# Seven block products of a gated feed-forward, accumulated in PSUM onto copies instead of added by VectorE

## The chip, the cores and the metric

One core of one Trainium2 chip. The metric is the device time of one execution in microseconds, median of three. In the texts, PE is TensorE (matmuls), PEld its weight loads, DVE is VectorE, ACT is ScalarE, POOL is GpSimd, SP the engine that issues most DMAs.

## The reference

```python
xn = layernorm(x)                              # x: 2048 x 512
s  = linear_attention(xn) @ wo                 # 32 heads of 16, dual softmax features
gate, up = xn @ W_gate, xn @ W_up              # 512 x 1376 each
h  = (gate * (gate > 0)) * up
out = x + s * silu(h @ W_down)                 # 1376 x 512
```

## The kernel before

All large products run in pairs of halves: every operand is split into a high part and a rest (`split`, L193: ScalarE writes the high part, VectorE or GpSimd subtracts to get the rest), and a product is three matmuls per block of the contraction (`mm3`, L198: rest times high, high times rest, high times high), accumulated in one PSUM bank of 128x512.

The kernel has three parts. First a loop over 16 tiles of 128 tokens: layer norm, transposes, the key, value and query projections, the feature map and the attention state. Then two passes (`half` 0 and 1, L1204), each over two blocks of 512 tokens. A pass walks 11 strips of the feed-forward width (`f` from 0 to 10, L1206). Each strip calls `gate_up(f)` (L558), which makes gate and up for both 512-token blocks. After the strips, a pass closes with the down projection of the last chunk of strips and the attention's output product (L1236 to L1276).

**`gate_up`.** Gate and up for the two token blocks form a 2x2 block product. The kernel uses seven block products instead of eight, on sums and differences of the inputs (A11, A12, A22, S1 to S4, kept in `XT`) and of the weights (`wa`, `wb`, `wc`, `wd`). Each product is two `mm3` steps, six matmuls of 512 columns. Before the change the order is: A11 into `pa`; S2 into `pb`; S3 into `pc`; S1 into `pd`; A22 onto `pc`; A12 onto `pa`; S4 onto `pd`. Three of them continue a bank that TensorE has written (`first=False`). What the banks must share is added by VectorE: a ScalarE copy `t1` of `pa`, then `m = pb + t1` (L571), `e7 = pc + m` (L582, or a ScalarE copy of `pc` when `copied`, that is in pass 1 from strip 2 on, with a GpSimd addition later, L593), `e7 = pd + e7` (L587), `pc = pc + m` (L594), `e7 = max(pc, 0) * e7` (L600), `m = pd + m` (L605) and `m = max(pa, 0) * m` (L606). The two results are split for the down projection; the split of the second one is put off (`LATE`) until the next strip's first product has been issued (`last_split`, L565). In a trace the tiles `t1`, `m` and `e7` show as `t`, `u` and `e`.

`gate_up` is a generator with seven yields, one after each product. `run` (L1186) steps through it, calls `pace.pump()` after each yield, and after the yields 3, 5, 6 and 7 issues one step of the down projection of earlier strips, if any is pending: two strips by three matmuls into a bank `py`, then an addition into `Y` (`y_sum`, L627: VectorE in pass 0, a ScalarE copy and GpSimd in pass 1). Such steps are pending in strips 2 to 9 of both passes, and not in the strips 0, 1 and 10: `CHUNKS` groups the strips by two, and `drain` (L1218) empties the list ahead of strip 10.

**What sets the order of the rest.** `Clock` (L62) keeps an estimate of when each engine is free, in TensorE cycles. `pump` issues pieces of other work (generators added with `pace.add`) when the estimate says that the engine is not more than `LIMIT` ahead. In pass 0 this is the preparation of the next strips' weights (`f_prep`, L479, on ScalarE and GpSimd, stored to HBM), the attention state (`state`, L1119: its results go over ScalarE as `XT<-kvt` and `zB<-pz`), and the queries (`q_pair`, L662: on VectorE a transpose `pq<-pql`, two reductions `mx`, two subtractions `eq`, later sums `qs`, reciprocals, two scalings `eq<-eq,qr` and transposes `ez` or `peT`; on ScalarE the exponentials and the copies `pTh`). In pass 1 the weights are reloaded from HBM and the queries go on. `InOrder` (L45) makes every engine issue in exactly the order in which the program was written, so whatever stands ahead of an instruction on its engine has to start first.

Of the kernel before, what the change touches and what calls it, by code (L numbers as in the profile page):

```python
# [13 lines left out]
P = 128  # L14
# [23 lines left out]
LATER = 9  # L38
START = (12, 15)
WO_WITH = (4, 5, 6, 7)  # L40

A21, A22, A11, A12, S1, S2, S3, S4 = range(8)

# [18 lines left out]
class Clock:  # L62
# [21 lines left out]
    def issued(self, key, name, a, k):  # L84
        o, ins = a[0], [*a[1:], *k.values()]
        n = max(x.free_size() for x in [o, *ins] if hasattr(x, "free_size"))
        start = max([self.now, *(self.there(x) + 200 for x in ins)])
        if name == "dma_start":
            self.ready[o.name] = start + self.LANDING
            if key == "gpsimd":  # L90
                self.free[key] = max(start, self.free[key]) + self.ISSUE
            return
        cost = self.RATE[key] * n
        if key == "tensor":
            n = o.free_size()
            cost = max(n, 245) + 30
            if name == "matmul" and a[2].dtype == F32:
                cost = n * 3 + 460
        if name == "reciprocal":
            cost *= 6  # L100
        self.free[key] = max(start, self.free[key]) + self.FIXED[key] + cost
        self.ready[o.name] = self.free[key] + (380 if key == "tensor" else 0)
# [56 lines left out]
def layer_kernel(ctx: ExitStack, tc: tile.TileContext, x, wkT, wqT, wv, wo, wf, cst, out):  # L159
# [46 lines left out]
            if i < n - 1:  # L206
                pace.pump()

    def transpose(o, src):
        nc.tensor.transpose(o, src, ident)  # L210

    def flat(e):
        return e.rearrange("p h s f -> p (h s f)")
# [29 lines left out]
    def fold(w, raw, k):  # L243

        p = ps(name="pfold")
        for j in range(KD):
            nc.tensor.matmul(p[:, j * P:(j + 1) * P], raw[:, j * P:(j + 1) * P], bd_sb[:, j, :],
                             start=True, stop=True)
        if w is WQ:
            return lambda: split(*w[k], p)  # L250
        return lambda: split(*map(by_parity, w[k]), even_first(p))
# [46 lines left out]
    def transpose_x(n):  # L298
        p = ps((P, 2, 2, P), name="pxT")
        xn = XN.pop(n)  # L300
        for k in range(KD):
            transpose(p[:, k // 2, k % 2, :], xn[:, k * P:(k + 1) * P])
        return p

    def xt_part(n, s):
# [58 lines left out]
    def query(n):  # L364


        h, d = divmod(n, 4)
        c = slice(h % 2 * 2 * P, (h % 2 + 1) * 2 * P)

        qs = [2 * b + h % 2 for b in PAIRS[h // 2][::-1]]  # L370
        p = ps((P, 2, 2 * P), name="pq")

        def w_of(d):
            return lambda k: [t[:, d * P:(d + 1) * P] for t in WQ[k]]
        if n < 2:
            i = 1 - n
            for d in range(2):
                mm3(p[:, d, :], w_of(d), lambda k: [XT[:, 2 * i + k // 2, s, k % 2, c] for s in range(2)], range(KD))
            to = [((qs[i], 0), slice(None), slice(None))]
        else:  # L380
            mm3(p, w_of(d), lambda k: [XT[:, k // 2:k // 2 + 3:2, s, k % 2, c] for s in range(2)], range(KD))
            to = [((q, d // 2), d % 2, i) for i, q in enumerate(qs)]
        t = u2((P, 2, 2 * P), "pqs")
        nc.scalar.activation(t, p, AF.Copy)
        for q, col, part in to:
            if q not in PQ:
                PQ[q] = dram((P, 2, 2 * P), f"pq{q[0]}{q[1]}")
            pace.when(t, lambda q=q, col=col, part=part: nc.sync.dma_start(PQ[q][:, col, :], t[:, part, :]))
# [166 lines left out]
    def a_of(c):  # L555
        return lambda k: (XT[:, c, 0, k, :], XT[:, c, 1, k, :])

    def gate_up(f, copied, used, halfway):  # L558

        pa = ps(name="pa")  # L560
        mm3(pa, w_of(f, 0, 0), a_of(A11), range(2))
        used(A11)
        t1 = u2((P, BT), "t1")
        nc.scalar.activation(t1, pa, AF.Copy)
        last_split()  # L565
        yield
        pb = ps(name="pb")
        mm3(pb, w_of(f, 1, 0), a_of(S2), range(2))
        used(S2)
        m = u2((P, BT), "u2")  # L570
        add(nc.vector, m, pb, t1)  # L571
        yield
        pc = ps(name="pc")
        mm3(pc, w_of(f, 1, 1), a_of(S3), range(2))
        FT[f][1] = None
        used(S3)
        halfway()
        e7 = u2((P, BT), "e7")
        if copied:
            nc.scalar.activation(e7, pc, AF.Copy)  # L580
        else:
            add(nc.vector, e7, pc, m)  # L582
        yield
        pd = ps(name="pd")
        mm3(pd, w_of(f, 2, 0), a_of(S1), range(2))
        used(S1)
        add(nc.vector, e7, pd, e7)  # L587
        yield
        mm3(pc, w_of(f, 2, 1), a_of(A22), range(2), first=False)
        FT[f][2] = None  # L590
        used(A22)
        if copied:
            add(nc.gpsimd, e7, e7, m)  # L593
        add(nc.vector, pc, pc, m)  # L594
        yield
        mm3(pa, w_of(f, 0, 1), a_of(A12), range(2), first=False)
        FT[f][0] = None
        used(A12)
        h1 = u2((P, BT), "hh", F32R), u2((P, BT), "hl", F32R)
        nc.vector.scalar_tensor_tensor(e7, pc, 0.0, e7, op0=ALU.max, op1=ALU.mult)  # L600
        split(*h1, e7, nc.gpsimd)
        yield
        mm3(pd, w_of(f, 3), a_of(S4), range(2), first=False)
        used(S4)
        add(nc.vector, m, pd, m)  # L605
        nc.vector.scalar_tensor_tensor(m, pa, 0.0, m, op0=ALU.max, op1=ALU.mult)  # L606
        h0 = u2((P, BT), "hh", F32R), u2((P, BT), "hl", F32R)
        LATE.append(lambda: split(*h0, m, nc.gpsimd))
        FT.pop(f)
        HS[f] = [h0, h1]  # L610
        yield
# [191 lines left out]
    def q_back(u, es, ez):  # L803

        (q, _), _ = UNITS[u]
        for j in range(2):
            th, tl = yield from turned_parts(u, es, ez, j, [(es[j], 0)])
            ez[j] = None
            yield "tensor", tl
            os_ = flat(es[j]).rearrange("p (a s t) -> p a s t", a=2, s=2)  # L810
            vh, vl = (t.rearrange("p (d t a x) -> p d a t x", d=2, a=2, x=32) for t in (th, tl))
            for a in range(2):
                p = ps((P, 2, 256), name="pnum")
                for s in range(2):
                    g = 4 * a + 2 * j + s
                    o = p[:, s, :].rearrange("p (t x) -> p t x", x=32)
                    mm(o, kvhl[:, 1, g, :], vh[:, s, a], True, False)
                    mm(o, kvhl[:, 0, g, :], vl[:, s, a], False, True)
                nc.scalar.activation(os_[:, a], p, AF.Copy)
            es[j] = None  # L820
            del th, tl, vh, vl
            DONE_Q[u] += 1
            STORES[u].append(pace.when(os_, lambda j=j, os_=os_: [o_store(q, j, s, os_[:, :, s, :]) for s in range(2)]))
        yield None,
# [361 lines left out]
    def run(g, per=1):  # L1186
        n = 0
        for _ in g:
            pace.pump()
            n += 1  # L1190
            if pending and n in (3, 5, 6, 7):
                if next(pending[0], pending) is pending:
                    pending.pop(0)
                    if pending:
                        next(pending[0])
                pace.pump()
# [7 lines left out]
    for half in range(2):  # L1204
        b0, b1 = 2 * half, 2 * half + 1
        for f in range(NF):  # L1206
# [21 lines left out]
            def used(c):  # L1228
                if half == 0 and f == NF - 1:
                    nc.sync.dma_start(f32(XT[:, c]), xt_spill[:, c - 1])  # L1230
            run(gate_up(f, half and f > 1, used, lambda: again and f_reload(f + 1, 1)))
            for c, fs in enumerate(CHUNKS[:-1]):
                if f == fs[-1]:
                    pending.extend(down((b0, b1)[j], j, fs, c == 0) for j in (1, 0))
# [7 lines left out]
        for j, b in enumerate((b1, b0)):  # L1242
            j = 1 - j
            if b == b0:
                for q in QUERIES[half][:2]:
                    o_split(q)
            parts = {}
            for i in range(TPB):
                if j == 1 and i < 3:
                    parts[i] = ps(name="py")  # L1250
                    down_rows(parts[i], i, j, fs[:-1], True, False)
            for i in range(TPB):
                if i in parts:
                    down_rows(parts[i], i, j, fs[-1:], False, True)
                else:
                    parts[i] = ps(name="py")
                    down_rows(parts[i], i, j, fs, True, True)
                y_sum(b, i, parts[i], False, True)
                y = Y[b][:, i, :]
                nc.scalar.activation(y, y, AF.Silu)  # L1260
                if b * TPB + i in yspill:
                    pace.when(y, lambda t=b * TPB + i, y=y: nc.sync.dma_start(yspill[t], y))
                pace.pump()
# [69 lines left out]
```

## Time and profile before

| what | us |
|---|---|
| median of three runs | 563.97 (563.05 to 564.35) |
| span of the profiled execution | 561.1 |
| start of the first strip of pass 1 in that span | 355.1 |
| last matmul in that span | 557.1 |

The profiled execution has no time of its own beside its span: 561.1 us lie between its first and its last instruction, 2.9 us less than the median of the runs. A change of the span is taken over to the median as it is. In the profile all instructions have line 58, that of the helper that records them, so they are told apart by their tiles: `pb<-XT,wb` is a matmul into `pb` from `XT` and `wb`. Rows of the timeline have the start in us, the duration in us, the engine, the operation, its tiles and shapes, how many instructions are merged in the row, and in brackets the idle time ahead of it and who ended it. Matmuls are pipelined: the duration of one row is longer than the distance to the next.

### The profile page before, as it was taken

What the parts mean: (1) busy time and instruction counts of PE and PEld (TensorE: products, weight loads), DVE (VectorE), ACT (ScalarE), POOL (GpSimd) and SP (SyncE); (2) the same over time, 40 slices, a digit from 0 to 9 for tenths busy, and PEclk for the clock granted to TensorE, in tenths of its full rate; (3) what the DMA queues carried; (4) which work ended last, traced back from release to release, by engine and by line L of the source; (5) the groups of instructions that cost most, each with busy time, mean ns of one, the idle gap of its engine ahead of it and who ended that gap; (6) DMA issues with size and microseconds to landing.
All of it is one profiled execution on the core that took longest, in us unless ns stands there. A gap on an engine that the chain in (4) does not pass through costs nothing.

```text
span 561.1 us, 8204 instructions
## 1 busy us (share of the span) xinstructions
PE 556.3 (99%) x2618; PEld 466.0 (83%) x2618; DVE 412.0 (73%) x623; ACT 282.7 (50%) x504; POOL 416.2 (74%) x356
## 2 busy tenths in 40 slices
PE   9999999999999999999999999999999999999997
PEld 8888888888888888888888888888888888888886
DVE  5978777677656898999798432699995959775324
ACT  3898687765545456444425251234463544534500
POOL 1689987898888386998889242572879788888474
PEclk9999999999999999999999999999999999999999
DMA  8349999765599827979767899997475666659675
GB/s 282 136 150 245 274 277 330 213 167 166 150 297 314 327 77 276 326 270 324 263 240 230 246 356 419 401 374 282 137 225 178 219 204 206 207 166 284 170 237 193
DMA packets 84538, 137.98 MB, mean 246 GB/s; under 512 B 7824, under 2 KB 34320, under 8 KB 83600
## 3 DMA queue, kind: packets, MB, share of 16 engines
q1 hardware_dynamic: 81040, 125.33, 65.1%
q0 software_dynamic: 3312, 12.06, 11.0%
q8 instruction: 21, 0.34, 0.3%
q14 instruction: 21, 0.17, 0.1%
q10 hardware_dynamic: 144, 0.07, 0.0%
HBM read 76.87 MB, written 52.69 MB: 231 GB/s over the span
## 4 chain that ended last, share of the span: by engine, by line
PE 99%; DVE 0%; issue 0%
PE py L58 21%; PE pc L58 11%; PE pa L58 11%; PE pd L58 11%; PE pv L58 8%; PE pk L58 8%; PE pq L58 8%; PE pso L58 8%; PE pb L58 5%; PE pkv L58 3%; PE pnum L58 3%; PE pxT L58 1%; PE pfold L58 1%; PE pidle L58 1%; PE pz L58 0%; DVE yk L58 0%
## 5 line engine op out<-in xcount | busy, mean ns | idle before, releaser
L58 PE MATMUL py<-fdh,hl 128*128 128x512 f32 x176 | 68.5, 389 | 0.0
L58 PE MATMUL py<-fdh,hh 128*128 128x512 f32 x176 | 68.5, 389 | 0.0
L58 PE MATMUL py<-fdl,hh 128*128 128x512 f32 x176 | 68.5, 389 | 0.0
L58 PE MATMUL pa<-XT,wa 128*128 128x512 f32 x264 | 67.4, 389 | 0.0
L58 POOL TENSOR_TENSOR hl<-e,hh 128x512 fp32r<-128x512 f32 x22 | 28.5, 1296 | 44.9 <-ACT hh L58 40.0
L58 PEld LDWEIGHTS pa<-XT,wa 128*128 128x128 f32 x264 | 49.5, 188 | 10.2
L58 ACT ACTIVATE hh<-e 128x512 fp32r<-128x512 f32 x22 | 13.9, 633 | 72.5 <-DVE e L58 70.1
L58 DVE TENSOR_TENSOR y<-py,y 128x512 f32<-128x512 f32 x40 | 27.5, 689 | 24.7 <-PE py L58 24.7
L58 POOL TENSOR_TENSOR phl<-ek,phl 128x1024 fp32r<-128x1024 f32 x15 | 36.1, 2409 | 11.1 <-ACT phl L58 11.1
L58 PE MATMUL pv<-wvh,XT 128*128 128x512 f32 x128 | 43.5, 401 | 0.0
L58 PE MATMUL pk<-wkh,XT 128*128 128x512 f32 x128 | 42.4, 392 | 0.0
L58 POOL TENSOR_TENSOR hl<-u,hh 128x512 fp32r<-128x512 f32 x22 | 28.8, 1311 | 16.6 <-ACT hh L58 14.3
L58 POOL TENSOR_TENSOR ez<-eq,zB 128x1024 f32<-128x1024 f32 x16 | 38.5, 2411 | 3.3 <-ACT eq L58 2.7
L58 PE MATMUL pq<-XT,wqh 128*128 128x512 f32 (+1 forms) x144 | 40.3, 366 | 0.0
L58 PEld LDWEIGHTS py<-fdh,hl 128*128 128x128 f32 x176 | 33.0, 188 | 6.9
L58 PEld LDWEIGHTS py<-fdh,hh 128*128 128x128 f32 x176 | 33.0, 188 | 6.8
L58 PEld LDWEIGHTS py<-fdl,hh 128*128 128x128 f32 x176 | 33.0, 188 | 6.8
L58 POOL TENSOR_TENSOR ol<-of,oh 128x512 fp32r<-128x512 f32 (+1 forms) x13 | 19.9, 1551 | 23.3 <-ACT oh L58 15.9
L58 PE MATMUL pc<-XT,wc 128*128 128x512 f32 x132 | 34.9, 392 | 0.0
L58 PE MATMUL pd<-XT,wc 128*128 128x512 f32 x132 | 33.8, 389 | 0.0
L58 PE MATMUL pc<-XT,wb 128*128 128x512 f32 x132 | 33.7, 389 | 0.0
L58 PE MATMUL pd<-XT,wd 128*128 128x512 f32 x132 | 33.5, 389 | 0.0
(162 smaller groups left out, 1581.0 us busy)
## 6 DMA issues: line engine op xcount, KB each, us to landing
zacc<-ek POOLq DMA_DIRECT2D x15, 512.0 KB, 6.0
xts<-XT SPq DMA_DIRECT2D x4, 1792.0 KB, 8.8
XT<-xts SPq DMA_DIRECT2D x7, 1024.0 KB, 19.6
wa<-ws SPq DMA_DIRECT2D x26, 256.0 KB, 5.0
wb<-ws SPq DMA_DIRECT2D x26, 256.0 KB, 4.4
wc<-ws SPq DMA_DIRECT2D x26, 256.0 KB, 5.0
ws<-wa SPq DMA_DIRECT2D x22, 256.0 KB, 4.5
ws<-wb SPq DMA_DIRECT2D x22, 256.0 KB, 4.2
```

What stands on the lines that cost most here:

```text
L58: return self.tc.keep_in_program_order(op(*a, **k))
```

## The change

Three additions of VectorE become accumulation. ScalarE copies `pa` (A11) into the bank `pb`, and S2 is accumulated onto that copy; ScalarE copies `pb` into the bank `pd`, and S1 and later S4 are accumulated there; VectorE adds S3, which ScalarE has copied to `t7`, once into `pb`, and A22 is accumulated onto the sum. `pa` is passed through ScalarE's Relu into `r`. The order of the products becomes A11 (`pa`), S3 (`pc`), S2 (`pb`), A12 (`pa`), S1 (`pd`), A22 (`pb`), S4 (`pd`). The steps of the down projection move to the yields 2, 4, 6 and 7. `halfway`, which reloads the second part of the next strip's weights, stays after the third product. The parameter `copied` and the GpSimd addition go.

Around it: the first matmul into a bank of several blocks alone has the start flag (`fold`, `transpose_x`, the first queries, `pnum`); a transpose is now written as a matmul with `is_transpose`, the same instruction; and `pump` is called three more times at the end of a pass.

```diff
+DOWNS = {2: 1, 4: 1, 6: 1, 7: 1}
...
-    def gate_up(f, copied, used, halfway):
+    def gate_up(f, used, halfway):
 
         pa = ps(name="pa")
         mm3(pa, w_of(f, 0, 0), a_of(A11), range(2))
         used(A11)
-        t1 = u2((P, BT), "t1")
-        nc.scalar.activation(t1, pa, AF.Copy)
+        pb = ps(name="pb")
+        nc.scalar.activation(pb, pa, AF.Copy)
         last_split()
-        yield
-        pb = ps(name="pb")
-        mm3(pb, w_of(f, 1, 0), a_of(S2), range(2))
-        used(S2)
-        m = u2((P, BT), "u2")
-        add(nc.vector, m, pb, t1)
         yield
         pc = ps(name="pc")
         mm3(pc, w_of(f, 1, 1), a_of(S3), range(2))
+        used(S3)
+        t7 = u2((P, BT), "t7")
+        nc.scalar.activation(t7, pc, AF.Copy)
+        yield
+        mm3(pb, w_of(f, 1, 0), a_of(S2), range(2), first=False)
         FT[f][1] = None
-        used(S3)
+        used(S2)
+        pd = ps(name="pd")
+        nc.scalar.activation(pd, pb, AF.Copy)
+        add(nc.vector, pb, pb, t7)
         halfway()
-        e7 = u2((P, BT), "e7")
-        if copied:
-            nc.scalar.activation(e7, pc, AF.Copy)
-        else:
-            add(nc.vector, e7, pc, m)
-        yield
-        pd = ps(name="pd")
-        mm3(pd, w_of(f, 2, 0), a_of(S1), range(2))
-        used(S1)
-        add(nc.vector, e7, pd, e7)
-        yield
-        mm3(pc, w_of(f, 2, 1), a_of(A22), range(2), first=False)
-        FT[f][2] = None
-        used(A22)
-        if copied:
-            add(nc.gpsimd, e7, e7, m)
-        add(nc.vector, pc, pc, m)
         yield
         mm3(pa, w_of(f, 0, 1), a_of(A12), range(2), first=False)
         FT[f][0] = None
         used(A12)
+        r = u2((P, BT), "r")
+        nc.scalar.activation(r, pa, AF.Relu)
+        yield
+        mm3(pd, w_of(f, 2, 0), a_of(S1), range(2), first=False)
+        used(S1)
+        add(nc.vector, t7, pd, t7)
+        yield
+        mm3(pb, w_of(f, 2, 1), a_of(A22), range(2), first=False)
+        FT[f][2] = None
+        used(A22)
         h1 = u2((P, BT), "hh", F32R), u2((P, BT), "hl", F32R)
-        nc.vector.scalar_tensor_tensor(e7, pc, 0.0, e7, op0=ALU.max, op1=ALU.mult)
-        split(*h1, e7, nc.gpsimd)
+        nc.vector.scalar_tensor_tensor(t7, pb, 0.0, t7, op0=ALU.max, op1=ALU.mult)
+        split(*h1, t7, nc.gpsimd)
         yield
         mm3(pd, w_of(f, 3), a_of(S4), range(2), first=False)
         used(S4)
-        add(nc.vector, m, pd, m)
-        nc.vector.scalar_tensor_tensor(m, pa, 0.0, m, op0=ALU.max, op1=ALU.mult)
+        add(nc.vector, r, pd, r, ALU.mult)
         h0 = u2((P, BT), "hh", F32R), u2((P, BT), "hl", F32R)
-        LATE.append(lambda: split(*h0, m, nc.gpsimd))
+        LATE.append(lambda: split(*h0, r, nc.gpsimd))
...
-            if pending and n in (3, 5, 6, 7):
+            for _ in range(DOWNS.get(n, 0)):
+                if not pending:
+                    break
...
-            run(gate_up(f, half and f > 1, used, lambda: again and f_reload(f + 1, 1)))
+            run(gate_up(f, used, lambda: again and f_reload(f + 1, 1)))
...
                     parts[i] = ps(name="py")
                     down_rows(parts[i], i, j, fs[:-1], True, False)
+                    pace.pump()
```

More of the change, by code (lines that the diff above doesn't have):

```diff
@@ L96, in issued @@
             cost = max(n, 245) + 30
-            if name == "matmul" and a[2].dtype == F32:
+            if name == "matmul" and a[2].dtype == F32 and not k.get("is_transpose"):
                 cost = n * 3 + 460
@@ L207, in mm3, with transpose @@
                 pace.pump()
-    def transpose(o, src):
-        nc.tensor.transpose(o, src, ident)
+    def transpose(o, src, start=True):
+        nc.tensor.matmul(o, src, ident, start=start, stop=True, is_transpose=True, skip_group_check=True)
     def flat(e):
@@ L246, in fold @@
         for j in range(KD):
-            nc.tensor.matmul(p[:, j * P:(j + 1) * P], raw[:, j * P:(j + 1) * P], bd_sb[:, j, :],
-                             start=True, stop=True)
+            mm(p[:, j * P:(j + 1) * P], raw[:, j * P:(j + 1) * P], bd_sb[:, j, :], j == 0, True)
         if w is WQ:
@@ L301, in transpose_x @@
         for k in range(KD):
-            transpose(p[:, k // 2, k % 2, :], xn[:, k * P:(k + 1) * P])
+            transpose(p[:, k // 2, k % 2, :], xn[:, k * P:(k + 1) * P], k == 0)
         return p
@@ L377, in query @@
             for d in range(2):
-                mm3(p[:, d, :], w_of(d), lambda k: [XT[:, 2 * i + k // 2, s, k % 2, c] for s in range(2)], range(KD))
+                mm3(p[:, d, :], w_of(d), lambda k: [XT[:, 2 * i + k // 2, s, k % 2, c] for s in range(2)], range(KD),
+                    d == 0)
             to = [((qs[i], 0), slice(None), slice(None))]
@@ L816, in q_back @@
                     o = p[:, s, :].rearrange("p (t x) -> p t x", x=32)
-                    mm(o, kvhl[:, 1, g, :], vh[:, s, a], True, False)
+                    mm(o, kvhl[:, 1, g, :], vh[:, s, a], s == 0, False)
                     mm(o, kvhl[:, 0, g, :], vl[:, s, a], False, True)
```

## The prediction, made before the change was run

> **What bounds the kernel now.** First the page: the busy row and the chain of work that ended last.
>
> ```profile
> span 561.1 us, 8204 instructions
> ...
> PE 556.3 (99%) x2618; PEld 466.0 (83%) x2618; DVE 412.0 (73%) x623; ACT 282.7 (50%) x504; POOL 416.2 (74%) x356
> ...
> PE 99%; DVE 0%; issue 0%
> ```
>
> TensorE is 99% of the chain: an engine that is faster elsewhere gains nothing unless TensorE waits for it. So the second view is the waits of the weight loads, which stand ahead of each matmul, and the third the timeline at the longest of them.
>
> ```profile
> PEld pc L58 <- DVE e L58: 0.7, 2, 0.4
> PEld pc L58 <- ACT e L58: 0.4, 1, 0.4
> ```
>
> ```profile
> 359.20 1.52 PE L58 MATMUL pd<-XT,wc 128*128 128x512 f32 x6
> ...
> 359.89 0.68 DVE L58 TENSOR_TENSOR e<-pc,u 128x512 f32<-128x512 f32 x1
> 360.04 1.28 ACT L58 ACT_TABLE_LOAD   x1 [2.77 <-DVE eq L58]
> 360.63 1.23 PEld L58 LDWEIGHTS pc<-XT,wc 128*128 128x128 f32 x6 [0.34 <-DVE e L58]
> 360.63 1.65 PE L58 MATMUL pc<-XT,wc 128*128 128x512 f32 x6
> ```
>
> Only three waits in the strips, and all in strips without down steps. What one costs: `pd`'s six matmuls end their turn 6 x 0.227 = 1.36 us after 359.20, at 360.56. VectorE's read of `pc`, which A22 waits for, ends at 360.57. A22 starts at 360.63 and takes 1.65 us instead of 1.52: 0.07 + 0.13 = 0.20 us lost by a release 0.01 us late. So a wait costs the lateness plus about 0.2 us, because the weight load can't run ahead. The other two cost about the same; all three are some 0.7 us. That is all that the strips can win.
>
> The pitch of 0.227 us is from two rows of the chain in order of time, 72 matmuls in 16.32 us each:
>
> ```profile
> 322.64 16.32 PE py L58 x72
> 338.96 16.32 PE pso L58 x72
> ```
>
> **The change part by part.** *TensorE's work.* In the order in which the two programs' instructions stand, TensorE has 2577 instructions in both, of the same shapes; the first that differs is the second product of the first strip. Start flags, and transposes written as matmuls, change no instruction's count or shape: 0 us.
>
> *VectorE, ScalarE, GpSimd.* VectorE loses 57 instructions of 0.68 us, 39 us; ScalarE gains 57, 34 us by its copies' 0.598 us; GpSimd loses 9, 12.7 us by its row. All of that lies beside a TensorE that is 99% of the chain: 0 us by itself.
>
> ```profile
> L58 ACT ACTIVATE t<-pa 128x512 f32<-128x512 f32 x22 | 13.2, 598 | 36.7 <-PE pa L58 36.5
> L58 DVE TENSOR_TENSOR u<-pb,t 128x512 f32<-128x512 f32 x22 | 15.0, 683 | 15.7 <-PE pb L58 9.5 <-ACT fdh L58 4.7 <-ACT hh L58 1.3
> L58 POOL TENSOR_TENSOR e<-e,u 128x512 f32<-128x512 f32 x9 | 12.7, 1406 | 5.3 <-DVE e L58 5.1
> ```
>
> A ScalarE copy from one bank into another is not in this trace. Its nearest row is the copy of `pa` to SBUF, 0.598 us, and I take that; the ends are 0.25 us (the shortest row of eight small copies, below) and 1.06 us (a copy of twice the columns, below). Over the two passes' 44 copies only those count that TensorE waits for, so the ends move the sum by -0.7 and +0.9 us with two or three such waits.
>
> *The new waits.* Before, TensorE waited in a strip for one thing: `pc` read by `e7`. Now there are four: S2 waits for ScalarE's copy `pb<-pa`; S1 for its copy `pd<-pb`; A22 for VectorE's addition into `pb`; S4 for VectorE's `t7 = pd + t7`. What lies between producer and consumer is one product (two for A22), and a down step where one is pending. Behind the waiting matmul is everything on TensorE, since its queue runs in order: each us late is a us of the span. How short one product is:
>
> ```profile
> 355.12 1.52 PE L58 MATMUL pa<-XT,wa 128*128 128x512 f32 x6
> ...
> 355.93 0.72 DVE L58 STREAM_TRANSPOSE pq<-pql 128x512 f32<-128x512 f32 x1
> 356.68 1.29 DVE L58 TENSOR_REDUCE mx<-pq 128x32 f32<-128x512 f32 x2
> 356.68 0.60 ACT L58 ACTIVATE t<-pa 128x512 f32<-128x512 f32 x1 [15.37 <-PE pa L58]
> ...
> 358.09 0.69 DVE L58 TENSOR_TENSOR u<-pb,t 128x512 f32<-128x512 f32 x1
> 358.70 0.68 DVE L58 TENSOR_TENSOR eq<-pq,mx 128x512 f32<-128x512 f32 x1
> 359.30 0.68 DVE L58 TENSOR_TENSOR eq<-mx,pq 128x512 f32<-128x512 f32 x1
> ```
>
> `pa`'s last matmul starts at 355.12 + 5 x 0.227 = 356.25; an idle ScalarE starts 0.43 us later and ends 1.03 us after that matmul's start. The product after the next is planned 7 x 0.227 = 1.59 us after it. So without a down step the slack is 1.59 - 1.03 - 0.2 = 0.36 us for ScalarE and, with 0.69 us, 0.27 us for VectorE; with a down step 1.36 us more. One foreign instruction ahead in the queue uses up the first; three the second. VectorE's instructions follow each other every 0.60 us (358.09, 358.70, 359.30, 359.89).
>
> *The queues in the changed program's order*, strip by strip, with these durations. Two places are far over their slack.
>
> (a) Pass 1, strip 0. VectorE's order is: addition into `pb`, then one transpose `pq`, two `mx`, two `eq` of the query, then `t7 = pd + t7`. S2's last matmul starts at 355.12 + 17 x 0.227 = 358.97; the copy `pd<-pb` runs 359.40 to 360.00; the addition 360.05 to 360.74. Then `pq` at 360.65, `mx` 0.75 us later (as 355.93 to 356.68), then every 0.60 us: `t7` runs from 363.8 to 364.5. S4 is planned at 355.12 + 6 x 1.36 = 363.28. Lost: 1.2 + 0.2 = **1.4 us**. If the query's five instructions weren't there it would be 0.
>
> (b) Pass 0, strip 1. ScalarE's order is `pb<-pa`, `hh<-r`, two `XT<-kvt`, `t7<-pc`, eight `zB<-pz`, and only then `pd<-pb`. Before, the same pieces ran here and nothing on TensorE waited:
>
> ```profile
> 177.28 1.52 PE L58 MATMUL pa<-XT,wa 128*128 128x512 f32 x6
> ...
> 178.84 0.60 ACT L58 ACTIVATE t<-pa 128x512 f32<-128x512 f32 x1 [1.99 <-PE pa L58]
> 179.33 0.62 ACT L58 ACTIVATE hh<-u 128x512 fp32r<-128x512 f32 x1
> ...
> 180.55 1.58 ACT L58 ACTIVATE XT<-kvt 128x1024 fp32r<-128x1024 f32 x2 [0.60 <-DVE kvt L58]
> ...
> 182.04 2.23 ACT L58 ACTIVATE zB<-pz 32x128 f32<-32x128 f32 x8
> 182.26 1.52 PE L58 MATMUL pd<-XT,wc 128*128 128x512 f32 x6
> ```
>
> With one VectorE instruction less ahead of `kvt`, `XT<-kvt` can start when `hh` ends, at 179.95, and runs to 181.5; `t7` to 182.0; `zB` 2.23 us to 184.2; `pd<-pb` to 184.7. S1 is planned at 177.28 + 4 x 1.36 + 0.91 (four matmuls `pz`) = 183.63. Lost: 1.1 + 0.2 = **1.3 us**.
>
> (c) The same bookkeeping in the other 20 strips gives four more that are over their slack by little: strips 1, 2 and 10 of pass 1 (0.3, 0.5, 0.7) and strip 7 of pass 0 (0.2), together **1.7 us**. In strip 10 the long copy `pTh` (1.06 us) of the last query stands ahead of `pd<-pb`, as it stood ahead of `e<-pc` in the trace:
>
> ```profile
> 505.77 1.06 ACT L58 ACTIVATE pTh<-ez 128x1024 fp32r<-128x1024 f32 x1 [0.52 <-DVE ez L58]
> 506.74 0.58 ACT L58 ACTIVATE e<-pc 128x512 f32<-128x512 f32 x1
> ```
>
> These hang on some tenths of a us; the four could be 0, and about as many others that I put just under the slack could be over it: 0 to 4 us.
>
> (d) In pass 0 `f_prep`'s copies wait on ScalarE for GpSimd, and behind them now stands `pd<-pb`:
>
> ```profile
> ACT woh L58 <- POOL wc L58: 4.9, 2, 3.7
> ACT wb L58 <- POOL tab L58: 3.9, 4, 1.8
> ACT fdh L58 <- POOL wa L58: 2.7, 1, 2.7
> ```
>
> With a down step in between the slack is 1.7 us, so the longest could cost 2 us; I take **0.5 us**, between 0 and 4.
>
> *Sum.* 1.4 + 1.3 + 1.7 + 0.5 - 0.7 = +4.2 us: a span of 565.3, and 563.97 + 4.2 = **568.2 us**.
>
> *DMAs and the end.* The reloads keep their place after the third product, and SP has the same 473 instructions. After the last strip of a pass A22 is now one product before the down steps need its split, not two; from A22's end a VectorE instruction, a ScalarE and a GpSimd one follow (0.7 + 0.6 + 1.3 us), while S4 and the 18 matmuls ahead of the first use give 1.36 + 4.08 us: 0 us, and 2 us if GpSimd has two instructions of 2.4 us ahead of it.
>
> **The rivals.**
>
> *No wait binds.* The three waits for ScalarE and VectorE fall inside the slack, because with 57 instructions less VectorE has no backlog when `t7`'s turn comes. This decides at (a): if `t7` has ended by 363.1, and in (b) `pd<-pb` by 183.4, only the gain is left: 563.97 - 0.7 = 563.3 us, not slower. For it: VectorE is idle ahead of a strip's own additions 9.5 us in total in the row of `u<-pb` above. Against it: in (a) and (b) the pieces are in the queue and can't be passed. 13%.
>
> *Many waits bind.* In pass 1 VectorE is late anyway. In the timeline S1's last matmul starts at 443.76 + 1.13 = 444.90, and VectorE reads `pd` only 3.3 us after it, the queue being full of `mx` and `eq`:
>
> ```profile
> 443.76 1.52 PE L58 MATMUL pd<-XT,wc 128*128 128x512 f32 x6
> ...
> 447.63 0.68 DVE L58 TENSOR_TENSOR eq<-mx,pq 128x512 f32<-128x512 f32 x1
> ...
> 448.23 0.69 DVE L58 TENSOR_TENSOR e<-pd,e 128x512 f32<-128x512 f32 x1
> ```
>
> Now S4 comes 13 matmuls after it (2.95 us), so such a lag costs 3.3 + 0.7 + 0.2 - 2.95 = 1.25 us. If half of the 16 strips with down steps lost that, 10 us: 568.2 - 2 + 10 = 576, of which (c) is a part. Against it: four of VectorE's own seven instructions remain, so the query's pieces come through earlier. I take half of it, 572, as its middle: 17%.
>
> *The clock drops.* In the first us of the span the granted pace is half:
>
> ```profile
> 1.06 5.06 PE L58 MATMUL pidle<-idle 128*128 128x128 f32 x22 [1.06 <-DVE mhalf L58]
> 6.86 3.77 PE L58 MATMUL pfold<-cb,wkT 128*128 128x128 f32 x32
> ```
>
> 0.23 us a matmul there, 0.118 us later. Were the new waits enough to bring that pace back for 5 us in (a) and in (b), each would cost 2.5 us: 573. The three waits of the trace were followed by no such stretch: six matmuls take 1.36 us on either side of them. 4%. [...]
>
> *TensorE gets a shorter pitch.* If VectorE's reads of the banks set the pitch, 57 fewer would shorten it. The rows of two stretches speak against it (columns after the length: busy time and count of PE, PEld, DVE, ACT and POOL, then the granted clock):
>
> ```profile
> 320.00:355.00 35.00, 35.00 (x156) 29.01 (x155) 11.70 (x17) 10.34 (x14) 10.55 (x6) 1.00 1.02 387
> 355.00:515.00 160.00, 160.00 (x707) 131.44 (x706) 134.14 (x192) 71.65 (x112) 122.90 (x82) 1.00 0.73 236
> ```
>
> VectorE is busy a third of the first and 84% of the second, and the pitch is the same: 16.32 / 72 in the first, 1.36 / 6 at 355.12 in the second. 2%. [...]
>
> **How the numbers follow.** Forecast (sum with one to three small waits more or less, 565.2 to 570.5): 64%; many waits 17%; none 13%; clock 4%; pitch 2%. A measurement of this kernel tells about 0.2%, 1.1 us, from no change: faster is below 562.8, slower above 565.1. Nearly all of "none" lies within, so faster 3%, same 14%, slower 83%. The range leaves out the lower part of "none" and the upper half of "many" and "clock": 564.2 to 573.0.
>
> **What would show it right or wrong.** In the changed profile the waits of the weight loads should name `pd <- DVE t` (a, S4) with a longest wait over 1 us, and `pd <- ACT pd` (b); the timeline near 363 should show `pq`, `mx`, `eq` between VectorE's `pb` and `t`, and near 184 eight `zB` ahead of `pd<-pb`. The pitch should stay 0.227 us. Wrong would be: no wait over 0.5 us, waits on weights (`wc<-ws`), which I put at nothing, or waits spread over most strips.

## The result and the profile after

| what | before | after |
|---|---|---|
| median of ten runs each, same chip | 563.98 us (562.41 to 564.42) | 565.25 us (564.60 to 565.71) |
| ratio | | 1.0026, 95% interval 1.0017 to 1.0035 |
| span of the profiled execution | 561.1 us | 563.9 us |
| its stretch from the first `pa` to the end of the last matmul | 390.6 us | 392.9 us |

The changed kernel is slower by 1.3 us (1.0 to 2.0), where 4.2 were forecast. A second comparison, on another chip, gave 565.05 against 563.37 us: 1.0031 (1.0019 to 1.0042). The long stretch in the last row holds both passes. It is the best figure for single steps, since it leaves out the start and the stores at the end: four profiles of the kernel before give 390.5 to 390.6 us for it, two of the changed one 392.9. So this stretch takes 2.3 us longer, 1.0 us more than the medians show. The shortest of the ten executions, 562.41 and 564.60 us, differ by 2.2 us; the kernel before scatters over 2.0 us, the changed one over 1.1.

First the page of the changed kernel: the span, the busy row, the chain.

```profile
span 563.9 us, 8200 instructions
...
PE 556.8 (99%) x2618; PEld 465.7 (83%) x2618; DVE 373.4 (66%) x566; ACT 312.8 (55%) x561; POOL 404.6 (72%) x347
...
PE 92%; DVE 3%; DMA 2%; ACT 1%; issue 1%; POOL 0%; SPq 0%; DVEq 0%; ACTq 0%
```

VectorE lost 38.6 us of work, and the time became longer: the chain, which was TensorE alone, now passes through VectorE and ScalarE. (Its DMA share is the load of the value weights in the first 17 us; a second profile of the kernel before has such a share too, 3%.) The waits of the weight loads name the places (total, times, longest):

```profile
PEld pd L59 <- ACT pd L59: 2.0, 2, 1.4
PEld pd L59 <- DVE t L59: 1.8, 2, 1.5
PEld pv L59 <- POOL wvl L59: 1.1, 2, 0.7
```

The first two rows are (b) and (a) of the prediction with one small companion each. The third lies in the first 21 us, ahead of the strips. It stood at 0.5 us in a second profile of the changed kernel and at 0.6 and 0.2 us in two of the kernel before: it varies from one execution to the next, in both kernels.

Place (b), the timeline of pass 0, strip 1:

```profile
182.60 2.21 ACT L59 ACTIVATE zB<-pz 32x128 f32<-32x128 f32 x8
...
182.99 1.52 PE L59 MATMUL pa<-XT,wa 128*128 128x512 f32 x6
...
184.84 0.58 ACT L59 ACTIVATE pd<-pb 128x512 f32<-128x512 f32 x1
...
185.47 1.65 PE L59 MATMUL pd<-XT,wc 128*128 128x512 f32 x6 [0.96 <-ACT pd L59]
```

The eight `zB` stand ahead of `pd<-pb`, which ends at 185.42. S1 was due at 182.99 + 6 x 0.227 = 184.35 and starts at 185.47. It then takes 1.65 instead of 1.52 us, because its weight loads couldn't run ahead (they start with it at 185.47, those of `pa` at 182.77, 0.22 us ahead of their matmuls): the distance from its first matmul to its second is 0.11 us above the pitch. Lost: 1.12 + 0.11 = 1.23 us.

Place (a), pass 1, strip 0:

```profile
362.02 0.70 DVE L59 TENSOR_TENSOR pb<-pb,t 128x512 f32<-128x512 f32 x1 [0.86 <-ACT pd L59]
...
362.62 0.72 DVE L59 STREAM_TRANSPOSE pq<-pql 128x512 f32<-128x512 f32 x1
...
363.92 1.52 PE L59 MATMUL pb<-XT,wc 128*128 128x512 f32 x6
...
365.18 0.68 DVE L59 TENSOR_TENSOR eq<-mx,pq 128x512 f32<-128x512 f32 x1
...
365.77 0.68 DVE L59 TENSOR_TENSOR t<-pd,t 128x512 f32<-128x512 f32 x1
...
366.51 1.66 PE L59 MATMUL pd<-XT,wd 128*128 128x512 f32 x6 [1.07 <-DVE t L59]
```

The query's five instructions stand between VectorE's two, as forecast. S4 was due at 363.92 + 1.36 = 365.28 and starts at 366.51: 1.23 + 0.11 = 1.34 us.

The other two losses are in pass 1: 0.11 us in strip 1 and 0.48 us in strip 10. No other strip has one: everywhere else the distance of the matmuls stays at the pitch.

### The profile page after: what moved, and what is told of

It reads as the page before. It is cut to its first block, busy times and chain, and to the rows that moved or that the text cites. A ratio compares the mean times of both kernels' runs of the same rounds, so it can differ in the third digit from the quotient of the medians.

```text
span 563.9 us, 8200 instructions
## 1 busy us (share of the span) xinstructions
PE 556.8 (99%) x2618; PEld 465.7 (83%) x2618; DVE 373.4 (66%) x566; ACT 312.8 (55%) x561; POOL 404.6 (72%) x347
## 4 chain that ended last, share of the span: by engine, by line
PE 92%; DVE 3%; DMA 2%; ACT 1%; issue 1%; POOL 0%; SPq 0%; DVEq 0%; ACTq 0%
PE py L59 21%; PE pd L59 10%; PE pa L59 10%; PE pb L59 10%; PE pq L59 8%; PE pso L59 8%; PE pv L59 7%; PE pk L59 7%; PE pc L59 5%; PE pkv L59 3%; PE pnum L59 2%; DMA wvr<-wv 2%; PE pxT L59 1%; DVE eq L59 1%; DMA xt<-x 1%
## 5 line engine op out<-in xcount | busy, mean ns | idle before, releaser
L59 POOL TENSOR_TENSOR hl<-t,hh 128x512 fp32r<-128x512 f32 x22 | 28.5, 1295 | 50.9 <-ACT hh L59 49.9
L59 DVE TENSOR_TENSOR pb<-pb,t 128x512 f32<-128x512 f32 x22 | 15.3, 697 | 45.9 <-ACT pd L59 45.9
L59 ACT ACTIVATE hh<-t 128x512 fp32r<-128x512 f32 x22 | 13.9, 633 | 53.6 <-DVE t L59 53.6
L59 POOL TENSOR_TENSOR hl<-r,hh 128x512 fp32r<-128x512 f32 x22 | 28.4, 1292 | 16.1 <-ACT hh L59 14.4
L59 POOL TENSOR_TENSOR y<-y,ys 128x512 f32<-128x512 f32 x24 | 30.9, 1293 | 9.6 <-ACT ys L59 9.6
```

The source lines that it names most:

```text
L59: return self.tc.keep_in_program_order(op(*a, **k))
```

## The experiments

Theory: the whole loss consists of waits of single strips for an instruction that stands in a full queue, each worth its lateness and about 0.1 us; most of what was forecast as (c) stayed away because VectorE has less to do. Rivals: the loss is spread (the longer path costs in every strip), it hangs on the engine that copies, or it comes from the start and not from the strips.

**1. The `zB` copies later.** They are held back until TensorE has been given two more matmuls' worth of columns (a third of a product), which puts `pd<-pb` ahead of them.

```diff
+            yield 2,
             for i in range(4):
                 r = slice(32 * i, 32 * i + 32)
                 nc.scalar.activation(zB[r, :, 32 * a:32 * a + 32], p[r, :, i, :], AF.Copy)
```

> The changed kernel, with ScalarE's eight copies zB of the attention state put off until pd<-pb of strip 1 of pass 0 has been issued. Queue theory (a wait costs what stands ahead of the copy on ScalarE): the 1.2 us that TensorE loses ahead of S1 in that strip go, and the span is 1.2 us shorter than the changed kernel's: 564.0 us against its 565.2. Rival (the loss is only moved: the copies held back make the queries later and TensorE waits somewhere else, or the added 1.3 us come from the accumulation itself): within 0.4 us of 565.2, with a new wait of about 1 us in the strips, or with none and no gain.

563.86 us, 1.0008 (0.9997 to 1.0018) of the kernel before. The waits of the weight loads in its profile:

```profile
PEld pd L59 <- DVE t L59: 1.8, 2, 1.5
...
PEld pd L59 <- ACT pd L59: 0.6, 1, 0.6
```

Of the waits for ScalarE that of strip 1 is gone, the one of strip 10 is left. The long stretch is 391.7 us, 1.2 less. Moving eight small copies gives back what (b) cost.

**2. The query later.** The queries of pass 1 start nine matmuls' worth of columns later (one and a half products).

```diff
-                queries = pace.add(all_queries(1), 5)
+                queries = pace.add(all_queries(1), 14)
```

> The changed kernel, with the queries of pass 1 begun 14 product columns of 512 after the pass's start instead of 5. VectorE then has two instructions of the query between its addition into pb and t7 = pd + t7 in strip 0, not five. Queue theory: the 1.3 us lost ahead of S4 in strip 0 go; strip 1 has a sum and a reciprocal there and may lose 0.3 us: 565.2 - 1.0 to 1.3 = 563.9 to 564.2 us. Rival (the backlog is only moved to the next strips): 565.2, with waits of together 1.3 us in strips 1 to 3 of pass 1.

563.85 us, 1.0009 (0.9999 to 1.0019). The same view of its profile:

```profile
PEld pd L59 <- ACT pd L59: 2.0, 2, 1.4
...
PEld pd L59 <- DVE t L59: 0.4, 1, 0.4
```

The 1.5 us for `t` are gone, 0.4 in strip 1 are left, where it was 0.3; the long stretch is again 391.7 us. In strip 0 two of the query's instructions still stand between VectorE's two and cost nothing. So (a) is that there were five. About 0.2 us of its 1.34 moved on to strip 1.

**3. Three places together.** Both edits, and in strip 10 of pass 1 VectorE copies `pb` to `pd`.

```diff
+        if half and f == NF - 1:
+            nc.vector.tensor_copy(pd, pb)
+        else:
+            nc.scalar.activation(pd, pb, AF.Copy)
```

> Both edits, and in strip 10 of pass 1 the copy pd<-pb on VectorE, so that ScalarE's pTh does not stand ahead of it (0.5 us). Queue theory: 1.2 + 1.3 + 0.5 less than the changed kernel, 562.2 us, and below the kernel before, which lost 0.7 us to its own three waits: 563.3 or less. Rival (the accumulation itself is slower, or the waits move): 565 us.

562.29 us (561.79 to 562.89) against 563.43 for the kernel before on the same chip: 0.9978 (0.9969 to 0.9987). This version beats both kernels. The waits, and strip 10 in the timeline:

```profile
PEld pd L59 <- DVE t L59: 0.4, 1, 0.4
```

```profile
505.87 1.06 ACT L59 ACTIVATE pTh<-ez 128x1024 fp32r<-128x1024 f32 x1 [0.70 <-DVE ez L59]
505.94 0.70 DVE L59 COPY pd<-pb 128x512 f32<-128x512 f32 x1
```

VectorE copies while ScalarE is busy with `pTh`, and S1 no longer waits. One wait is left of all four; the stretch is 390.1 us, 2.8 below the changed kernel and 0.55 below the kernel before. The scheme itself is cheap; the three meetings in the queues made it dear. Of the 1.14 us by which the median beats the kernel before, the stretch shows only half; the rest lies outside it, as above. A loss spread over all strips, or one from the start, is out with these three experiments.

**4. The down steps where they were.** After the yields 3, 5, 6 and 7.

```diff
-DOWNS = {2: 1, 4: 1, 6: 1, 7: 1}
+DOWNS = {3: 1, 5: 1, 6: 1, 7: 1}
```

> The changed kernel, with the steps of the down projection back at the yields 3, 5, 6 and 7. Between pa and S2, and between S2 and S1, then lies one product of 1.36 us and no down step in the strips 2 to 9 of both passes, and ScalarE has one or more foreign instructions ahead of its copies in most of them. Queue theory: a wait of 0.3 to 1.5 us at one or both places in most of these 16 strips, 8 to 20 us more: 573 to 585 us. Rival (ScalarE is idle at these points, so that the slack was not needed): under 2 us more, 565 to 567 us.

567.80 us, 1.0082 (1.0067 to 1.0097): 2.6 us above the changed kernel, and the stretch as well (395.5 us). That is far less than the 8 to 20 us that the bookkeeping of the queues had put, and more than the rival's 2. Three new waits for `pb<-pa` came, all in pass 1, here the longest in the total and strip 4 in the timeline:

```profile
PEld pb L59 <- ACT pb L59: 2.3, 3, 1.2
```

```profile
411.94 1.05 ACT L59 ACTIVATE eq<-eq 128x1024 f32<-128x1024 f32 x1
...
412.89 0.58 ACT L59 ACTIVATE y<-py 128x512 f32<-128x512 f32 x1
...
413.37 0.59 ACT L59 ACTIVATE pb<-pa 128x512 f32<-128x512 f32 x1
...
414.01 0.53 PEld L59 LDWEIGHTS pb<-XT,wb 128*128 128x128 f32 x3 [1.23 <-ACT pb L59]
```

Without a down step between S3 and S2, an exponential and a copy ahead of `pb<-pa` are enough. That only 3 of the 16 strips with down steps met such a queue there, and one more (in pass 0) ahead of `pd<-pb`, is why the step was overestimated; the new places of the down steps are worth about 2.6 us all the same. The three cost 1.9 us, the one for `pd` 0.4, a new wait of `pnum` for VectorE's `pTl` 0.6; the loss in strip 10 of pass 1, 0.5 us, went.

**5. Both copies on VectorE.**

```diff
-        nc.scalar.activation(pb, pa, AF.Copy)
+        nc.vector.tensor_copy(pb, pa)
...
-        nc.scalar.activation(pd, pb, AF.Copy)
+        nc.vector.tensor_copy(pd, pb)
```

> The changed kernel with both copies, pb<-pa and pd<-pb, made by VectorE instead of ScalarE. Computes the same. If the queue of the engine that makes the copy is what counts: the waits in strip 1 of pass 0 (1.23 us, ScalarE behind eight zB) and in strip 10 of pass 1 (0.48 us, ScalarE behind pTh) go, 1.7 us; VectorE gets 44 instructions of 0.6 to 0.7 us more, about what the change had taken from it, so its lag in pass 1 grows again; where its lag ahead of a copy is over about 0.7 us in a strip without down steps, or 2 us in one with them, new waits pb<-DVE or pd<-DVE come: 2 to 5 us. Together 565.5 to 568.5 us, waits named DVE only. If only the engine's speed counts (VectorE reads these shapes in 0.68 us, ScalarE in 0.58 us): within 0.5 us of the changed kernel's 565.25.

570.79 us (570.75 to 572.11), 1.014 (1.0122 to 1.0158); more than either theory gave, though the waits are of the kind expected, for VectorE alone:

```profile
PEld pd L59 <- DVE pd L59: 4.6, 3, 2.9
PEld pb L59 <- DVE pb L59: 3.6, 2, 2.5
```

The longest, in the timeline of strip 3 of pass 1:

```profile
400.41 1.22 DVE L59 TENSOR_REDUCE qs<-ez 128x64 f32<-128x1024 f32 x1 [2.40 <-POOL ez L59]
401.55 0.69 DVE L59 COPY pd<-pb 128x512 f32<-128x512 f32 x1
402.14 0.69 DVE L59 TENSOR_TENSOR pb<-pb,t 128x512 f32<-128x512 f32 x1
402.29 2.20 PEld L59 LDWEIGHTS pd<-XT,wc 128*128 128x128 f32 x6 [2.88 <-DVE pd L59]
```

The reduction `qs` waits 2.40 us for GpSimd, and behind it in VectorE's queue stands the copy that TensorE needs. The expectation had counted VectorE's load, not what VectorE itself waits for. (Ahead of the second longest, 2.5 us, it is VectorE's own work: two scalings that take 2.34 us.) ScalarE is the better choice by some 5.5 us here, and by its queue more than by its speed: the five waits for copies add up to 8.2 us, where a copy takes 0.58 us on ScalarE and 0.69 us on VectorE.

**6. VectorE's load given back.** Two copies per strip that nothing reads, after S3 and after A22; the order of all other instructions stays.

```diff
         nc.scalar.activation(t7, pc, AF.Copy)
+        tc.keep_in_program_order(tc.nc.vector.tensor_copy(dead, pc))
...
         used(A22)
+        tc.keep_in_program_order(tc.nc.vector.tensor_copy(dead, pb))
```

> The changed kernel with two copies by VectorE in every strip that nothing uses (of pc after the second product, of pb after the sixth): 44 instructions of about 0.65 us, 29 of the 39 us that the change takes from VectorE, with no other instruction moved. Theory, that the small waits of strips 1, 2 and 10 of pass 1 and 7 of pass 0 stayed away because VectorE had less to do: VectorE's lag at t<-pd in pass 1 grows back towards that of the kernel before (1.3 to 3.8 us in strips 1 to 10), and waits pd<-DVE t or pb<-DVE pb come in several strips: 567 to 571 us. Rival, that they were put too high for another reason (the copies' durations, the slack): the added work fits into VectorE's idle time, no new wait over 0.3 us, 565.0 to 566.0 us.

569.86 us, 1.012 (1.0103 to 1.0138); the stretch is 397.8 us, 4.9 above the changed kernel. Its added work, by group (busy us, mean ns), and its waits:

```profile
L573 DVE CAST dead<-pc 128x512 bf16<-128x512 f32 x22 | 15.0, 683 | 27.1 <-ACT t L59 27.1
L596 DVE CAST dead<-pb 128x512 bf16<-128x512 f32 x22 | 14.9, 678 | 3.2 <-PE pb L59 3.2
```

```profile
PEld pd L59 <- DVE t L59: 3.2, 3, 1.9
PEld pd L59 <- ACT pd L59: 3.1, 3, 1.5
PEld pb L59 <- DVE pb L59: 1.4, 1, 1.4
```

The losses per strip are, beside (a) and (b): strip 7 of pass 0 1.9 us, strips 1, 2 and 10 of pass 1 0.1, 0.8 and 1.0 us. Those are just the four strips that the prediction named under (c), though strip 1 loses no more than without the copies. Strip 3 of pass 0 adds 0.3, and (a) grows by 0.4 us. In strip 10 the wait is for ScalarE's `pd<-pb`, although only VectorE got work: VectorE's `ez` comes later, ScalarE's `pTh` after it, and the copy behind that. The copies could also delay by waiting themselves: in the first row VectorE stands idle for 27.1 us ahead of them. But in strip 7 of pass 0 and in strip 2 of pass 1 it has no idle time between the copy and the late instruction, so there it is their work. The theory holds; the added work doesn't fit into idle time for free.

**7. A second copy in the path.** ScalarE copies `pb` once more ahead of `pd<-pb`.

```diff
+        tc.keep_in_program_order(tc.nc.scalar.activation(dead, pb, AF.Copy))
         nc.scalar.activation(pd, pb, AF.Copy)
```

> The changed kernel with one more copy of pb by ScalarE, which nothing uses, ahead of pd<-pb in every strip: 22 instructions of about 0.58 us, each in the path from S2 to S1. Theory of the slack (0.36 us in a strip without down steps, 1.7 us with one, and a restart of 0.1 to 0.2 us): the six strips 0, 1 and 10 of both passes lose, four of them 0.58 - 0.36 + 0.11 = 0.33 us each, strip 1 of pass 0 and strip 10 of pass 1, which wait already, 0.58 us each: 2.5 us, 567.7 us, and none of the 16 strips with down steps waits. Rival, that the path binds in every strip: 22 x 0.58 = 12.8 us, 578 us. Rival, that S1 doesn't hang on the copy's end at all: 565.3 us.

567.92 us, 1.0084 (1.0069 to 1.0099), as expected from the slack (567.7) and far from 578. Two rows of its waits and strip 10 of pass 0 in its timeline:

```profile
PEld pd L59 <- ACT pd L59: 3.6, 4, 1.9
PEld pd L59 <- DVE t L59: 2.5, 2, 1.9
```

```profile
319.97 0.59 ACT L59 ACTIVATE pd<-pb 128x512 f32<-128x512 f32 x1
...
320.67 0.30 PEld L59 LDWEIGHTS pd<-XT,wc 128*128 128x128 f32 x2 [0.36 <-issue]
```

That the sum was right is luck, for its parts weren't all. Of the four strips that had just been in time three lost 0.15 to 0.21 us each and one nothing, instead of 0.33 each: the copy comes 0.55 us later and S1 by 0.04 to 0.13 us, so the slack is 0.1 to 0.2 us larger than worked out. In exchange S4 became later by 0.4 us in each of strips 0 and 1 of pass 1 and by 0.5 us in strip 7 of pass 0, because VectorE's addition into `pb` and all behind it wait for the copy too. In the 16 strips with down steps S1 waits in none.

**8. The kernels once more.** The changed kernel with three rounds, and three more profiles of the kernel before.

> The changed kernel once more. If the 0.8 us that its profile lost before 24.5 us (value projections waiting for a load's split on GpSimd) came by chance, another profile has less of it there and the same 392.9 us from the first pa to the last matmul, and the time stays between 564.6 and 565.7 us with a clock of 0.999 to 1.000. If it belongs to the change, the wait comes again.

565.05 us, 1.0031; stretch 392.9 us; the wait at the start was there again, 0.5 us instead of 1.1.

> The kernel before, once more, for its profile: its times lie between 562.4 and 565.2 us, and the profile known is of one near the low end. If the difference between its executions lies in the start (what the first 30 us wait for), the stretch from the first pa to the last matmul takes 390.6 us again. If it lies in the granted clock (0.998 in most of its long executions, 0.999 to 1.000 in the short ones), that stretch is longer by up to 1 us and a slower pitch shows in some stretch.

562.92 us, granted clock 1.000, stretch 390.6 us.

> The kernel before, for a profile of one of its long executions (about one in three shows a clock of 0.998 and 563.8 to 565.2 us). If the clock is it, the matmuls run for some 2 us at half pace in some stretch, which the profile then shows; a short execution takes 390.6 us from the first pa to the last matmul again.

563.21 us, granted clock 0.998: of the kind looked for, though not a long one. The stretch is 390.5 us as always. The clock is missing only after the last matmul, in the windows from there to the end, first of this execution, then of the one above (length, busy of PE, PEld, DVE, ACT, POOL, granted clock, DMA share, GB/s):

```profile
557.20:561.40 4.20, 0.01 (x1) 0.00 (x0) 1.18 (x3) 0.00 (x0) 0.00 (x0) 0.73 0.66 246
```

```profile
557.50:561.10 3.60, 0.06 (x1) 0.00 (x0) 0.85 (x2) 0.00 (x0) 0.00 (x0) 1.00 0.58 215
```

The 0.998 is thus no slower TensorE: its clock falls when its work is done, and the end takes 4.2 instead of 3.6 us. In the four profiles of the kernel before the end takes 3.6, 3.6, 3.7 and 4.2 us, in the nine of the changed kernel and its variants 3.5 us each.

> As the one before it: a second draw for a long execution of the kernel before.

562.71 us, clock 1.000, stretch 390.6 us: a short one again. An execution at 564 us or more wasn't caught in a profile.

## Why the prediction was right in direction and wrong in size

*TensorE's work, and what lies beside it: 0 us.* Right: the same 2618 matmuls in both profiles (the prediction's 2577 is its count in the programs, which no profile shows), and no stretch with another pitch.

*(a) 1.4 us and (b) 1.3 us.* Right: 1.34 and 1.23 us, at the place, for the engine and behind the very instructions named; experiment 2 takes away (a) alone and experiment 1 (b) alone. The two waits that the prediction gave as its signs are the first two rows of the profile after.

*(c) 1.7 us: the first step that failed.* It measured 0.59: strip 1 0.11 instead of 0.3, strip 2 nothing instead of 0.5, strip 10 0.48 instead of 0.7, strip 7 of pass 0 nothing instead of 0.2. The mechanism is right, the size isn't. Strip 2 shows it, in the changed kernel's timeline:

```profile
388.72 0.68 DVE L59 TENSOR_TENSOR t<-pd,t 128x512 f32<-128x512 f32 x1
...
389.91 1.52 PE L59 MATMUL pd<-XT,wd 128*128 128x512 f32 x6
```

For a loss of 0.5 us `t` would have had to end 0.3 us after 389.91. It ended at 389.40: the bookkeeping had VectorE 0.8 us later than it was. With 30 us of work given back (experiment 6) `t` starts 2.9 us after S1's last matmul instead of 1.75, and S4 waits 0.99 us:

```profile
392.36 0.68 DVE L59 TENSOR_TENSOR t<-pd,t 128x512 f32<-128x512 f32 x1
...
393.09 0.99 PEld L59 LDWEIGHTS pd<-XT,wd 128*128 128x128 f32 x5 [0.99 <-DVE t L59]
```

The sum entered VectorE's lost 39 us as "0 us by itself". Experiment 6 shows that they are worth something, as slack: with 30 of them given back three of the four strips of (c) lose 3.8 us together instead of 0.48. The prediction had this as an argument of its rival "no wait binds" and gave it no term in the sum. Whether its bookkeeping left out this relief, or was wrong elsewhere, is not shown: it gives its results strip by strip, not its working.

*(d) 0.5 us: the second step that failed, 0.* Its premise was that `pd<-pb` stands behind ScalarE's waits for GpSimd. The 2.7 us for `fdh`, the second longest of its three rows, lie in the loop over the tokens, long before the first strip:

```profile
68.98 0.63 ACT L58 ACTIVATE fdh<-rawd 128x512 fp32r<-128x512 f32 x1 [2.75 <-POOL wa L58]
```

And of the waits that are left in pass 0 of the changed kernel the long ones, 2.85 and 1.41 us, come after the strip's `pd<-pb`, not ahead of it. The longest, and then strip 4, where ScalarE is furthest behind when S2 ends:

```profile
242.02 0.58 ACT L59 ACTIVATE pd<-pb 128x512 f32<-128x512 f32 x1
...
246.88 0.63 ACT L59 ACTIVATE woh<-wor 128x512 fp32r<-128x512 f32 x1 [2.85 <-POOL wd L59]
```

```profile
226.91 0.60 ACT L59 ACTIVATE pd<-pb 128x512 f32<-128x512 f32 x1
...
229.58 1.52 PE L59 MATMUL pd<-XT,wc 128*128 128x512 f32 x6
```

The copy starts 0.76 us later there than behind an idle ScalarE and ends at 227.51, 2.07 us ahead of S1. The query's four `pnum` matmuls, 0.9 us, stand in between beside the down step, but it would have been in time without them. The least that is left in any strip of pass 0 with a down step is 1.3 us (strip 3).

*The old waits, -0.7 us.* Right and a little more: all of them are gone, 0.67 us in the strips and 0.16 us of a `pnum` wait for GpSimd.

*The sum.* 1.34 + 1.23 + 0.59 + 0 - 0.83 = +2.3 us, which is what the long stretch shows. Of the 1.9 us by which the forecast exceeds that, 1.6 are (c) and (d). The medians show only +1.3 and +1.7. The rest, 0.6 to 1.0 us, lies outside this stretch, and it is the third step that failed: to take the change of the span over to the median as it is. The time of an execution is about 1.8 us more than its span in the runs on record, so the profile before, 561.1 us, was of one of about 562.9 us, 1.1 below the median: the kernel before has executions over 564 us that its four profiles, with spans of 560.9 to 561.4 us, don't represent. Experiment 8 points to the end of the program, by 0.6 us in one execution; what makes the longest ones stays open. So of the 2.9 us between forecast and measurement 1.1 are (c), 0.5 are (d), 1.0 is the step from span to median, and the rest is spread over the other terms.

*The rivals.* "No wait binds" fell with (a) and (b), though it was right on 18 of the 22 strips. "Many waits" is refuted for this kernel, with four strips of 22 that lose anything, but experiment 6 shows how near it was: with three quarters of the work given back the kernel takes 4.6 us more. The clock did not fall: 0.999 granted, 0.227 us pitch, and six matmuls after a wait of 1.2 us take 1.65 us, of which only the first distance is longer. (The half pace of the first microseconds, 0.23 against 0.118 us a matmul, from which the prediction worked out its price, is read from the distances in its rows; the granted clock in the window from 0 to 6 us reads 1.00.) In waits of this length and number no fall is seen; the last section has a run where the clock fell in a longer one, of 2.9 us. The pitch did not shorten with 57 fewer reads of the banks by VectorE: 72 matmuls take 16.32 us in both profiles.

## What to carry to other kernels

When work is taken from an engine that isn't the bound, look for what TensorE newly waits for: list each producer, what stands ahead of it in its queue, and how many matmuls lie between. Place the producer or move what is ahead of it, three small edits here, before judging the scheme: the same change was 0.26% slower or 0.22% faster depending on three places (in the long stretch, 2.3 us slower or 0.55 us faster). In such a sum let the freed time shorten the queues, and before pricing another engine's wait look up where it stands: ahead of the instruction that TensorE needs, or behind it. And compare the profiled execution's time with the median before adding a change of the one to the other.

## What the runs showed of the hardware

ScalarE's copy from one PSUM bank to another takes 582 to 587 ns for 128x512, somewhat less than the 598 ns that its copy to SBUF took before; VectorE's in experiment 5 takes 0.69 us. The groups of the changed kernel:

```profile
L59 ACT ACTIVATE pd<-pb 128x512 f32<-128x512 f32 x22 | 12.9, 587 | 9.6 <-PE pb L59 9.5
L59 ACT ACTIVATE pb<-pa 128x512 f32<-128x512 f32 x22 | 12.8, 582 | 36.6 <-PE pa L59 36.6
```

In one wait the clock came down. In the profiled execution of experiment 5 the last matmul ahead of the wait for `pd` has its turn until 399.68, the next starts at 402.29, and those behind it come every 0.43 us instead of 0.227, for some 3 us. No other of the thirteen profiles has such a stretch. It takes 0.003 off the granted clock of the whole span, which is 0.996 here and 0.999 to 1.000 in eleven of the others; the one with 0.998 (experiment 8) loses that after its last matmul, at 0.73 for 4.2 us. The windows there (third column from the end: the granted clock):

```profile
399.68:401.90 2.22, 0.15 (x1) 0.00 (x0) 1.49 (x2) 0.60 (x1) 2.22 (x2) 1.00 1.02 344
401.90:402.29 0.39, 0.00 (x1) 0.00 (x1) 0.39 (x2) 0.00 (x0) 0.39 (x1) 0.51 0.94 362
402.29:405.31 3.02, 3.02 (x7) 2.44 (x8) 2.88 (x6) 0.00 (x0) 0.39 (x1) 0.50 0.26 96
```

So the clock is full for 2.2 us of the idle time and then at half until 405.31. The 3.0 us of matmuls at half pace cost 1.5 us, and this execution is 1.3 us longer than the other three (572.11 against 570.75 to 570.83), whose clock is 1.000. A wait of 2.5 us in the same execution (the second row of its waits; granted clock 1.00 in the window from 431 to 436) and all waits up to 1.9 us in the other runs were followed by no such stretch. The clock fell 2.2 us into the longest wait; in the wait of 2.5 us TensorE stood still for 2.26 us (431.48 to 433.74) without a fall. So the length of a wait alone doesn't decide it here; what else does stays open.
